# Attention and a silu MLP in one kernel: score units of the late visits one place earlier, one couple's q in rows of its own, late weight loads issued by GpSimd

## The chip, the cores and the metric

The kernel runs on one core of one Trainium2 chip. The metric is device time in microseconds (us). Engines are named as in the profile: PE is TensorE's matmul, PEld its weight load, DVE is VectorE, ACT is ScalarE, POOL is GpSimd, and SP is SyncE, which only issues DMAs. `L706` is line 706 of the kernel before.

## The reference

The inputs are `q`, `k`, `v` (8 batches, 12 heads, 448 tokens, 64 wide), two gains, and the weights `w_in` (768 x 2048) and `w_out` (2048 x 768), all float32.

```python
q_n, k_n = rmsnorm(q, g_q), rmsnorm(k, g_k)          # over the 64 of a head
attn = softmax(q_n @ k_n.T / sqrt(64))               # per batch and head
x = (attn @ v).transpose(0, 2, 1, 3).reshape(3584, 768)
h = x @ w_in                                         # 3584 x 2048
out = (h * sigmoid(h)) @ w_out                       # 3584 x 768
```

## The kernel before

**Couples.** Attention is done in 24 couples of four heads each (two pairs of heads of one batch); three couples make a batch, and six couples (`GROUP`) a group of two batches, whose x is then multiplied by w_in. The code counts couples from 0, so that couple 8 of the change's short name is `c = 7` in the code; the code's count is used from here on. The main loop is

```python
for c in range(NC):
    visit(c)
    between(c)
visit(NC)
```

**A visit** holds the attention of couple c. It has seven score units, `scores(c, j, i)` for j = 0, 1, 2 (blocks of 128 keys) and i = 0, 1 (the pair), and one for the 64 keys left over (`LEFT`). A unit is four matmuls (L701) into a PSUM tile named `sc`, of which there are two, and the exponentials on ACT (L706). The products with v, `weigh(c, j, step)`, are matmuls (L738) into two PSUM banks, `av0` and `av1`, one of each. A visit begins by finishing the couple before: the last products of c-1, a small copy into a bank (`turn`, L714), and `divide(c-1)` (L796, DVE), which multiplies the banks by the reciprocals of the softmax sums and so writes x. Only after the divide may the first products of couple c enter the banks. "Late" visits are those with c of 6 and more; in the earlier ones PE transposes q and k.

**Between two visits** lie, on PE, mostly the products of w_in with the x of a previous group (L870, PSUM tiles `mm`, two of them), a fast matrix multiplication with seven products for eight. Their sums go through DVE (L828), POOL (L890, L891) and ACT (L888, L1008), and the finished blocks are saved to a DRAM tensor `hidden` (SP, L903) from whose landing on a staging tile is free again. Other steps are dealt out among these products, in an order that the program writes out by hand; there is no planner:

- `add` (L752, DVE) and `sum_up` (L772 PE, L781 DVE): sums of the exponentials and their reciprocals, which SP then spreads over the partitions by DMAs (L787, L789).
- `flip(c+1, "q")` and `flip(c+1, "k")` (L644, L647, DVE): transposes of the next couple's q and k. After the flip of q, its rows are free, and the flip issues the next loads into them (`load_q`, L249, eight DMAs of 56 KB on SP).
- `sum_squares(c+2)` (ACT L661, DVE L662) and `scale(c+2)` (PE L673, DVE L674, POOL L677 and L680): the RMS norm of the q of the couple after the next, in place.
- the norm of k (ACT L458, DVE L459 and L483, POOL L487).
- `weights_in`: a piece of w_in, 128 x 512, is rounded. A `Rounder` loads it (L84), ACT splits it (L99, L100), DVE rounds (L122, L125, L129) and POOL adds (L133); at the end of a rounding the next loads are issued whose raw tile is free. A raw tile is free after the rounding before it that used it.
- `sum_x` (L825, DVE): sums of x that the fast multiplication needs, once a group and bank half.

Each engine takes its instructions in the order of the program. Between(c) for c = 6 and up holds 52 or 56 product matmuls. Couple c's q lies in `q_of(c)`: two sets of rows in turn for c below 6, one alone, `rows_q[0]`, from 6 on:

```python
def q_of(c):
    return rows_q[c % 2 if c < GROUP else 0]
```

So in between(5), q(6) is flipped, q(7) is loaded over it, and then squared and scaled before visit 6. After all visits the rest of the w_in products follow, and from 890 us on the products with w_out (L1177, L1214), which the change doesn't touch.

Of the kernel before, what the change touches and what calls it, by code (L numbers as in the profile page):

```python
# [17 lines left out]
I64 = mybir.dt.int64  # L18
# [45 lines left out]
class Rounder:  # L64
# [3 lines left out]
    def __init__(self, nc, pieces):  # L68
        self.nc = nc
        self.pieces = pieces  # L70
        self.loaded = self.opened = self.rounded = 0

    def load(self):

        i = self.loaded
        if i == len(self.pieces):
            return False
        dst, src, raw, low = self.pieces[i]
        if raw[0] is not None and raw[0] >= self.rounded:
            return False  # L80
        self.loaded += 1
        raw = raw[1]
        if src.dtype == I64:
            self.nc.sync.dma_start(raw.bitcast(I64), src)  # L84
        return True

    def open(self):
# [439 lines left out]
def bounded(  # L527
# [10 lines left out]
    NC, loads, place, norm, spare, ones, first, squares = (  # L538
        own[name] for name in ("NC", "loads", "place", "norm", "spare", "ones", "first", "squares")
    )  # L540
    GROUP = z.NPAIR
# [45 lines left out]
        return own["second_q"] if c == 1 else raw_q[c % 2]  # L587

    def q_of(c):
        return rows_q[c % 2 if c < GROUP else 0]  # L590

    def load_q(c):

        if 0 < c < NC:
            loads["q"](c, raw_of(c) if c < GROUP else q_of(c))
# [15 lines left out]
    def transpose_q(c):  # L611

        t = ps.tile([P, 2, BANK], F32, name="sc", bufs=2)
        both = [t[:, i] for i in range(2)]
        if c == 0:
            both[1] = ps.tile([P, BANK], F32, name="av1")
        for i in range(2):
            for j in range(J):
                rows = q_of(c)[0:R, ts(i * J + j, 2 * D)]
                nc.tensor.transpose(both[i][:, ts(j, R)], rows, ident[0:R, 0:R])  # L620
            if c == 0:
                (nc.scalar.copy, nc.vector.tensor_copy)[i](qT[:, i], both[i][:, 0:S])
        if c > 0:
            nc.scalar.copy(qT, t[:, :, 0:S])
        if c == GROUP - 2:
            load_q(GROUP)

    def transpose_k(c):

# [11 lines left out]
    def flip(c, name):  # L641

        if name == "q":
            nc.vector.transpose(qT.rearrange("p i s -> p (i s)"), q_of(c)[:, 0 : z.NK])  # L644
            load_q(c + 1)
            return
        nc.vector.transpose(kT, place["k1"])  # L647
        if c + 1 < NC:
            loads["quarters"](c + 1)
# [7 lines left out]
    def sum_squares(c):  # L657

        if c >= NC:
            return  # L660
        nc.scalar.activation(squares, q_of(c)[:, 0 : z.NK], AF.Square)  # L661
        nc.vector.tensor_reduce(  # L662
            out=norm.rms[c % 2][:, 0:n], in_=squares.rearrange("p (n e) -> p n e", e=z.Q),
            axis=AX.X, op=ALU.add,
        )
# [26 lines left out]
    def scores(c, j, i=None):  # L692


        two = ps.tile([P, 2, BANK], F32, name="sc", bufs=2)
        for half in range(2):
            pair = half if j == LEFT else i
            keys = kT[:, ds((z.KA, z.KB)[0 if j == LEFT else i] + j * P, P)]
            for h in range(2):
                rows = ds(h * D, D)  # L700
                nc.tensor.matmul(  # L701
                    two[ds(half * D, D), h, 0:S], keys[rows, ts(half, D)], qT[rows, pair, :],
                    start=True, stop=True,
                )
        for h in range(2):
            nc.scalar.activation(  # L706
                eleft[:, h] if j == LEFT else weights(c, j)[:, i, h], two[:, h, 0:S], AF.Exp,
                scale=norm.column(c, i, h, j),
            )
# [638 lines left out]
    def weights_in(c, half):  # L1348
        i = 2 * (c - GROUP) + half
        work = [step_of[step] for step in ("ro" if c < GROUP else halves.get(i, ""))]  # L1350
        return work + [lambda a=a: sum_w_in(*a) for a in sums_halves.get(i, ())]
# [10 lines left out]

    def visit(c):

        if c < GROUP - 1:
            beside = normalise(c + 1)
        elif c == GROUP - 1:
            beside = [lambda: sum_squares(c + 1), lambda: scale(c + 1)] + normalise(c + 1)[2:]
        else:
            beside = []  # L1370
        if c < NC:
            scores(c, 0, 0)
        run_all(beside[0:1])
        if c > 0:
            weigh(c - 1, LEFT)
            weigh(c - 1, LEFT - 1, 0)
            turn(1, nc.scalar.copy if c < GROUP else nc.vector.tensor_copy)
        if c < NC:
            scores(c, 0, 1)
        if c == 0:  # L1380
            run_all(beside[1:2])
        if c > 0:
            weigh(c - 1, LEFT - 1, 1)
            if c - 1 < EARLY:
                for i in range(2):
                    nc.vector.tensor_copy(x_of(c - 1, i), sums[i])
                run_all(beside[1:2])
                if inverting:
                    if c > 1:
                        divide(c - 2, None)  # L1390
                    run_all(inverting)
                    inverting.clear()
            else:
                divide(c - 1, sums)
                run_all(beside[1:2])
                if c < NC and c % GROUP == 0:
                    for i in range(0 if c == GROUP else 1, HW):
                        sum_x(last_two(c), i)
                weights_in_visit(c)
            if c + 1 < NC:  # L1400
                loads["vrest"](c + 1)
        if c == NC:
            return
        scores(c, 1, 0)
        scores(c, 1, 1)
        if c < GROUP:
            run_all(beside[2:3])
        weigh(c, 0, 1)
        scores(c, 2, 0)
        weigh(c, 1, 1)  # L1410
        turn(0, nc.scalar.copy)
        if c < GROUP:
            run_all(beside[3:4])
        scores(c, 2, 1)
        weigh(c, 0, 0)
        run_all(add(c, 1))
        weigh(c, 1, 0)
        scores(c, LEFT)
        if c + 1 < NC:
            loads["v"](c + 1)  # L1420

    def run_all(work):
        for piece in work:
            piece()

    def between(c):

        def transposes_and_sums():
            summing = sum_up(c)
            if c < GROUP:  # L1430
                next(summing)
            if c < GROUP - 1:
                transpose_k(c + 1)
            reciprocals = next(summing)
            if GROUP - 1 <= c < NC - 1:
                reciprocals += [lambda: flip(c + 1, "k"), gain]
            if GROUP // 2 <= c <= EARLY:
                divide(c - 1, None)
            return reciprocals

        if c < GROUP - 1:
            transpose_q(c + 1)
        elif c < NC - 1:
            flip(c + 1, "q")
        if c < GROUP // 2:
            inverting.extend(transposes_and_sums())
        elif c == GROUP - 1:
            run_all(transposes_and_sums())
        if c >= GROUP and c % GROUP == 0:
            fetched = range(AHEAD) if c == GROUP else ()  # L1450
            columns = products - 2 * HW * S * len(fetched)
            work = halves_in(last_two(c), range(HF), plain_in, dict(begun), fetched)
            begin(work, columns, 2 * GROUP)
            begun.clear()
        late = add(c, LEFT - 1) + add(c, LEFT) if c >= GROUP else []
        further = normalise(c + 2)[2:] if c >= GROUP - 1 else []
        queries = [lambda: sum_squares(c + 2)] if c >= GROUP - 1 else []
        fill(late + weights_in(c, 0) + further)
        prompt = transposes_and_sums() if GROUP // 2 <= c != GROUP - 1 else []
        if c == GROUP // 2:  # L1460
            begin(make_ahead([0, 1]), AHEAD * 2 * HW * S, GROUP - 1)
        fill(weights_in(c, 1), prompt[:3] + [lambda: run_all(prompt[3:] + queries)])
        if c == GROUP - 2:
            pair_up()
        if c % GROUP == GROUP - 1:
            finish()
            if c == GROUP - 1:
                begun[0] = fetch_ahead([0, 1], 0)
            else:
                sum_x([c // GROUP * 2, c // GROUP * 2 + 1], 0)  # L1470
        if c >= GROUP - 1:
            scale(c + 2)
        if GROUP <= c < NC - 1:

            nc.scalar.activation(first, minus_half, AF.Exp)
        if c == NC - 1:
            while rounder.load():
                pass
# [236 lines left out]
```

## Time and profile before

| what | value |
|---|---|
| median of 3 runs | 1343.11 us (1342.66 to 1343.29) |
| profiled execution, own time | 1346.0 us |
| its span | 1344.1 us |
| mean granted PE clock of it | 0.994 |
| busy PE / DVE / ACT / POOL | 1300.4 / 951.8 / 502.3 / 369.5 us |
| visit 6 | 131.36 to 144.79 us |
| visit 7 | 168.85 to 179.85 us |
| visit 8 | 203.38 to 214.36 us |
| visit 9 | 243.42 to 254.40 us |

The visits' times are from PE's timeline: from the first matmul of unit (0, 0) on. The profile comes from one execution, and its times are from the span's start. In a timeline a row has start, length, engine, line, operation, output <- input, and in brackets how long the engine was idle before it and what released it. "SPq" rows are DMAs being issued, which takes SP's time; the transfer lands later. The clock of PE is granted by a throttle, and a matmul at half clock takes about twice as long.

### The profile page before, as it was taken

To read this page: it belongs to the slowest core of one execution; us is meant where nothing else is said; L and a number is where in the kernel's file an instruction comes from. 1 tells how busy PE (TensorE), PEld (TensorE's weight loads), DVE (VectorE), ACT (ScalarE), POOL (GpSimd) and SP (SyncE) were. 2 spreads that over 40 slices of the span, in tenths; PEclk is the share of its full clock that TensorE was granted. 3 is DMA by queue.
4 is the path that set the end of the run, shared out by engine and by line. 5 is a ranking of instruction groups with operands and counts; after the bars stand their busy time and mean duration, and the time that the engine had idled before them with its cause. 6 is when DMAs were issued, how large, how long until landed. Compare 5 with 4: busy or idle time off the path is not lost.

```text
span 1344.1 us, 19812 instructions
## 1 busy us (share of the span) xinstructions
PE 1300.4 (97%) x7111; PEld 828.3 (62%) x7111; DVE 951.8 (71%) x1630; ACT 502.3 (37%) x877; POOL 369.5 (27%) x223
## 2 busy tenths in 40 slices
PE   8997998999999999999999999999999999999997
PEld 4332443444444444444444455557999999999997
DVE  5786876785855655855554586789978787878785
ACT  7874455556445545455544244420000000101000
POOL 5765344443343343343331044410000000000000
PEclk9998999999999999999999999999999999999999
DMA  8565456434433543443421257422323232332311
GB/s 230 155 147 123 119 155 161 106 89 109 108 91 88 124 93 87 124 97 86 112 74 38 101 176 262 149 98 71 103 75 99 75 102 77 99 100 79 125 48 39
DMA packets 286543, 147.69 MB, mean 110 GB/s; under 512 B 224420, under 2 KB 270372, under 8 KB 286436
## 3 DMA queue, kind: packets, MB, share of 16 engines
q1 hardware_dynamic: 285872, 145.35, 39.6%
q8 instruction: 58, 0.95, 0.3%
q0 software_dynamic: 256, 0.79, 0.2%
q14 instruction: 49, 0.40, 0.1%
q10 hardware_dynamic: 308, 0.20, 0.0%
HBM read 96.73 MB, written 41.29 MB: 103 GB/s over the span
## 4 chain that ended last, share of the span: by engine, by line
PE 81%; DVE 7%; ACT 4%; DMA 3%; issue 2%; SPq 2%; POOL 0%; ACTq 0%; DVEq 0%
PE mm L870 24%; PE alone L1177 22%; PE av L738 8%; PE sc L701 8%; PE mm L1177 7%; PE alone L870 7%; PE alone L1214 2%; DVE work L781 1%; DVE work L752 1%; DMA rows<-in_k_dram 1%; PE sc L772 1%; SPq L249 1%; DVE sums_x L825 1%; PE mm L1214 1%; ACT L1008 1%
## 5 line engine op out<-in xcount | busy, mean ns | idle before, releaser
L870 PE MATMUL mm<-x,W 128*128 128x448 f32 x636 | 258.6, 549 | 12.0 <-DVE parts L828 3.3
L706 ACT ACTIVATE work<-sc,rms 128x448 f32<-128x448 f32 x324 | 185.5, 635 | 86.2 <-PE sc L701 62.8
L870 PEld LDWEIGHTS mm<-x,W 128*128 128x128 f32 x636 | 117.6, 191 | 146.8 <-issue 114.7
L870 PE MATMUL mm<-sums_x,W 128*128 128x448 f32 x456 | 186.5, 548 | 6.8 <-DVE parts L828 4.8
L701 PE MATMUL sc<-work 64*64 64x448 f32 x1344 | 167.3, 550 | 1.7 <-DVE rms L674 1.1
L738 PE MATMUL av<-work,rows 64*64 64x448 f32 x1296 | 156.0, 546 | 4.7 <-ACT av L714 1.8
L752 DVE TENSOR_TENSOR work<-work 128x896 f32<-128x896 f32 (+1 forms) x114 | 123.7, 1115 | 49.4 <-PE av L738 48.8
L870 PEld LDWEIGHTS mm<-sums_x,W 128*128 128x128 f32 x456 | 85.1, 191 | 100.2 <-issue 83.4
L487 POOL TENSOR_TENSOR rms<-rms,minus_half 128x14 f32<-128x14 f32 (+3 forms) x37 | 88.3, 2389 | 134.6 <-DVE rms L483 133.9
L514 POOL DMA_DIRECT2D out_dram<-x x2 | 1.3, 652 | 443.0 <-DVE x L828 443.0
L1177 PE MATMUL alone<-W,rows 128*128 128x192 f32 x608 | 113.0, 326 | 0.0
L738 PEld LDWEIGHTS av<-work,rows 64*64 64x64 f32 x1296 | 60.7, 133 | 76.0 <-issue 35.4
L677 POOL TENSOR_TENSOR rms<-rms,minus_half 128x28 f32<-128x28 f32 x18 | 86.2, 4791 | 74.7 <-DVE rms L674 63.3
L1177 PEld LDWEIGHTS alone<-W,rows 128*128 128x128 f32 x608 | 101.2, 190 | 0.0
L701 PEld LDWEIGHTS sc<-work 64*64 64x64 f32 x1344 | 55.5, 134 | 69.1 <-ACT work L706 26.9
L890 POOL TENSOR_TENSOR parts<-parts,stage 128x448 f32<-128x448 f32 x31 | 42.0, 1355 | 150.3 <-DVE parts L828 149.9
L1177 PE MATMUL alone<-W,work 128*128 128x192 f32 x382 | 72.2, 326 | 0.0
L1008 ACT ACTIVATE stage<-stage 128x896 f32<-128x896 f32 x63 | 57.4, 947 | 24.7 <-DVE stage L828 24.1
L1177 PEld LDWEIGHTS alone<-W,work 128*128 128x128 f32 x382 | 63.8, 190 | 0.0
L1187 ACT COPY rows<-alone 128x192 f32<-128x192 f32 x34 | 10.9, 320 | 137.4 <-PE alone L1177 78.9
L781 DVE RECIPROCAL work<-sc 128x224 f32<-128x224 f32 x36 | 55.6, 1547 | 5.2 <-PE sc L772 5.0
L459 DVE TENSOR_REDUCE rms<-rows 128x8 f32<-128x512 f32 (+2 forms) x48 | 30.2, 629 | 40.3 <-ACT rows L458 37.5
(243 smaller groups left out, 2104.9 us busy)
## 6 DMA issues: line engine op xcount, KB each, us to landing
hidden<-stage SPq DMA_DIRECT2D x63, 448.0 KB, 3.1
work<-hidden SPq DMA_DIRECT2D x21, 1024.0 KB, 5.1
rows<-in_moe_w_out_dram SPq DMA_DIRECT2D x32, 384.0 KB, 3.4
W<-in_moe_w_in_dram SPq DMA_DIRECT2D x22, 512.0 KB, 5.0
work<-work SPq DMA_DIRECT2D x144, 56.0 KB, 2.0
rows<-in_q_dram SPq DMA_DIRECT2D x144, 56.0 KB, 2.3
rows<-in_k_dram SPq DMA_DIRECT2D x144, 56.0 KB, 2.4
x<-hidden SPq DMA_DIRECT2D x7, 1024.0 KB, 5.6
```

The costliest lines, as they stand in the source:

```text
L487: nc.gpsimd.tensor_tensor(out=t, in0=t, in1=half, op=ALU.pow)
L677: nc.gpsimd.tensor_tensor(out=f, in0=f, in1=minus_half.to_broadcast([P, n]), op=ALU.pow)
L701: nc.tensor.matmul(two[ds(half * D, D), h, 0:S], keys[rows, ts(half, D)], qT[rows, pair, :], start=True, stop=True,)
L706: nc.scalar.activation(eleft[:, h] if j == LEFT else weights(c, j)[:, i, h], two[:, h, 0:S], AF.Exp, scale=norm.column(c, i, h, j),)
L738: nc.tensor.matmul(sums[i][ds(h * D, D), :], v, w, start=(j == 0 and step == 1), stop=(j == LEFT - 1 and step == 1),)
L752: nc.vector.tensor_tensor(out=total, in0=total, in1=more, op=ALU.add)
L781: nc.vector.reciprocal(out=r[0][:, rows], in_=t[:, rows])
L870: nc.tensor.matmul(t, self.left(name, s), self.right(name, s), start=s == ends[0], stop=s == ends[1])
L890: nc.gpsimd.tensor_tensor(out=u2, in0=u2, in1=p5, op=ALU.add)
L1008: nc.scalar.activation(t, t, AF.Silu)
L1177: nc.tensor.matmul(t, x[:, i], y, start=i == ORDER[0], stop=i == ORDER[-1])
L1214: nc.tensor.matmul(o, a[:, 2 * i + m, t], right_one(name, i)[:, m], start=n == 0, stop=n == len(steps) - 1,)
```

## The change

It has three parts.

1. In late visits `scores(c, 1, 0)` is issued before the last product of couple c-1 (and so before the divide), and `scores(c, 2, 0)` before the first product of couple c. PE's order before was: 00, two products of c-1, 01, last product of c-1, 10, 11, product 0, 20, product 1, 21, and so on. Now: 00, two products of c-1, 01, 10, last product of c-1, 11, 20, product 0, product 1, 21.
2. Couple 7's q goes to the second set of rows, which is free by then, and is loaded in between(4). Its squares and scale are no longer at the end of between(5); they are dealt among the first products of between(6), with `sum_squares` where the flip of q(7) stood, and that flip comes late in between(6), after the flip of k. In between(5) the flip of q(6) is followed by the load of q(8).
3. From visit 6 on, the loads of w_in (seven into W tiles and two into an x tile, 512 KB each) are issued by POOL instead of SP, directly after POOL's rounding instruction in POOL's order.

```diff
@@ class Rounder
+        self.queue = nc.sync
...
-            self.nc.sync.dma_start(raw.bitcast(I64), src)
+            self.queue.dma_start(raw.bitcast(I64), src)
@@ def q_of(c)
-        return rows_q[c % 2 if c < GROUP else 0]
+        return rows_q[c % 2 if c < GROUP + 2 else 0]
@@ def transpose_q(c)
-        if c == GROUP - 2:
-            load_q(GROUP)
+        if c >= GROUP - 2:
+            load_q(c + 2)
@@ def flip(c, name)
-            load_q(c + 1)
+            if c != GROUP + 1:
+                load_q(c + 2 if c == GROUP else c + 1)
@@ def visit(c)
+        if c == GROUP:
+            room.w_in.queue = nc.gpsimd
...
+        if GROUP <= c < NC:
+            scores(c, 1, 0)
         if c > 0:
             weigh(c - 1, LEFT - 1, 1)
...
-        scores(c, 1, 0)
+        if c < GROUP:
+            scores(c, 1, 0)
         scores(c, 1, 1)
         if c < GROUP:
             run_all(beside[2:3])
+        if c >= GROUP:
+            scores(c, 2, 0)
         weigh(c, 0, 1)
-        scores(c, 2, 0)
+        if c < GROUP:
+            scores(c, 2, 0)
@@ def between(c)
+            if c == GROUP:
+                reciprocals.insert(3, lambda: flip(c + 1, "q"))
...
-        elif c < NC - 1:
+        elif c < NC - 1 and c != GROUP:
             flip(c + 1, "q")
...
-        queries = [lambda: sum_squares(c + 2)] if c >= GROUP - 1 else []
-        fill(late + weights_in(c, 0) + further)
+        queries = [lambda: sum_squares(c + 2)] if c >= GROUP else []
+        prompt = [lambda: sum_squares(c + 1), lambda: None, lambda: scale(c + 1)]
+        fill(late + weights_in(c, 0) + further, prompt if c == GROUP else [])
...
-        fill(weights_in(c, 1), prompt[:3] + [lambda: run_all(prompt[3:] + queries)])
+        n = max(3, len(prompt) - 1)
+        fill(weights_in(c, 1), prompt[:n] + [lambda: run_all(prompt[n:] + queries)])
...
-        if c >= GROUP - 1:
+        if c >= GROUP:
             scale(c + 2)
```

## The prediction

> **What bounds the kernel now.** I read the page's busy times first, then TensorE's waits in the stretch that the change touches, then the queues behind those waits.
>
> ```profile
> PE 1300.4 (97%) x7111; PEld 828.3 (62%) x7111; DVE 951.8 (71%) x1630; ACT 502.3 (37%) x877; POOL 369.5 (27%) x223
> ```
>
> TensorE (PE) is the bound. The change adds and removes no matmul, so only time in which PE waits, or runs at half clock, can move. After 760 us the two programs are alike. PE's waits between 100 and 345 us, in total, count and longest:
>
> ```profile
> PE mm L870 <- DVE parts L828: 7.0, 6, 2.0
> PE mm L870 <- DVE stage L828: 4.7, 6, 1.2
> PE sc L673 <- DVE rms L662: 4.7, 3, 3.9
> PE mm L870 <- ACT stage L888: 3.2, 2, 2.5
> PE mm L870 <- DVE work L781: 2.4, 1, 2.4
> ```
>
> The 3.9 us is couple 7's sum of squares, late at the end of between(5). PE's timeline (start, length, instruction, idle before):
>
> ```profile
> 122.76 4.12 PE L870 MATMUL mm<-x,W 128*128 128x448 f32 x6 [2.38 <-DVE work L781]
> 130.80 0.62 PE L673 MATMUL sc<-rms,ident 128*128 128x28 f32 x2 [3.92 <-DVE rms L662]
> 131.36 1.03 PE L701 MATMUL sc<-work 64*64 64x448 f32 x4
> ```
>
> The 2.5 us at L888 lies in between(8). SP's timeline there, then ACT's line from the timeline of all engines:
>
> ```profile
> 213.00 3.51 SPq L84 DMA_DIRECT2D W<-in_moe_w_in_dram  x2
> 219.65 2.31 SPq L303 DMA_DIRECT2D rows<-in_v_dram  x4
> 222.05 4.07 SPq L249 DMA_DIRECT2D rows<-in_q_dram  x8
> 226.22 0.90 SPq L903 DMA_DIRECT2D hidden<-stage  x2
> ```
>
> ```profile
> 229.50 0.53 ACT L888 COPY stage<-mm 128x448 f32<-128x448 f32 x1 [8.56 <-DMA hidden<-stage]
> ```
>
> Until 216.6 SP is at w_in loads that wait for roundings on POOL (SP's waits name L133: 14.5 us in four waits from 100 to 345 us). The v and q loads and the save of `hidden` queue behind them. The save is issued at 226.22 though its activation ended near 219.8; L888 waits for it, L458 and L459 wait behind L888, and a product behind L459 costs PE another 2.02 us at 234.62.
>
> In the late visits themselves little is lost: 11.00 us (visit 7) against 28 rounds of four matmuls side by side, 0.376 us each, 10.52. That is 0.45 to 0.51 per visit; visits 12 and 18 lose 1.31 and 1.26.
>
> **What the Trainium skill says.** "TensorE: Matmul & The Clock Gate", Part 1, gives a free-running window of 3413 ns after which an idle PE runs at half clock. The trace agrees: the records show half clock from 122.64 to 126.05, from 129.47 to 136.29 and from 235.28 to 238.69, one or two such windows each, after the waits shown. "SBUF — State Buffer", section "SBUF: two separate sides", calls the port pair of VectorE and GpSimd an exclusive lock, and its box warns that a DMA of the POOL queue has descriptors made by GpSimd, which the lock can keep waiting. Of the first the trace shows L125, 0.43 us mostly and up to 1.80; of the second only POOL's stores at the kernel's end, 0.54 to 0.76 us each.
>
> **Part 1, couple 7's q.** L661, L662, L673 and L674 leave between(5). Its last products then end at 122.76 + 4.12 = 126.9, and visit 6 starts there, 4.5 us sooner than 131.36; the second half-clock window (131.36 to 136.29 inside the visit, worth 2.46) goes too.
>
> Three things take some back. SP issues q(8)'s eight loads (0.52 us each, some 4.2 to 4.9 in all) in the slot of q(7)'s, but q(7)'s eight have gone in earlier, into a queue nearly without gaps from 99 to 129. So the spreading of couple 5's reciprocals (L787, L789) comes that much later: the last L789, issued by 128.9 before, is issued near 132 to 133 and landed at about 134.5. The divide (L796, 137.90 before) can't start sooner; PE would have its banks full at 132.5, and waits some 1.7 us at the first product into a bank not yet divided. The score unit moved forward waits for the first exponential, behind L99 and L100 on ACT (0.4), and a product waits for the copy L714 behind DVE's rounding (0.6). Visit 6: 126.8 + 10.5 + 0.45 + 0.4 + 0.6 + 1.7 = 140.4, where it ended at 144.8: **4.4 ahead**.
>
> In between(6) the work comes back. After the divide, DVE has the sums of x and the adds to 144.4; ACT squares after the last exponentials (144.5 to 145.45), L662 ends at 146.6, L828 and two L752 follow, and L674 ends at 150.3. POOL then works in order. Durations are those of POOL's groups:
>
> - L677 4.8, L680 1.7, L133 1.3, w_in load 0.65 (the stores' price), L890 1.14: together 9.6.
>
> L890 thus ends at about 160.0. The L828 that waits for it started at 158.78 before, now at 160.1: 1.3 later. PE has two product buffers and idles about 4 us meanwhile. Behind that L828 stands what it had behind it, plus the flip of couple 7's q (L644), 1.10, which stood at 148.9. Visit 7 therefore starts 1.3 + 1.1 = **2.4 later** than 168.85, less 0.1 for DVE's idle spots: +2.3. So 4.4 us won at the visit's end are lost in the stretch. Bounds: −2, if the spreading is not late and the chain starts with it; +5, if the load's descriptors wait for DVE (the box gives about 3.1 us for one beside a VectorE copy; no run here shows it) and PE falls to half clock.
>
> **Part 2, w_in loads by POOL.** Seven W and two x loads of 512 KB go. SP is rid of the wait for L133, since POOL issues the load after its own rounding. In between(8) the v and q loads and the save run through, and L888 comes about 22 us after visit 8's start at 203.38, some 4 before its 26.1. The wait of 2.55 goes; of 2.02 stay about 1.6; the half-clock window, 1.7, goes; and of the 1.03 at 221.7 some 0.4. In sum 2.55 + 0.4 + 1.7 + 0.4 = **−5.1**; from −2.5 (another engine late next: DVE, busy 27 of 40 us there) to −5.5. On POOL a load costs 0.65 ahead of L890, with POOL 27% busy it hides, but for between(6) above. Landing (5.0 before) may grow by the issue; the load is needed two roundings later, so at nothing; if that cover is gone, PE waits for a rounding, 1 to 2 us.
>
> **Part 3, score units forward.** Nothing is added. In a visit, unit 20 comes 1.5 us sooner and waits for the exponential of 10 to free its "sc" buffer (+0.28), while two staggers (0.2 at the product 11, 0.1 at 00 behind L714) vanish: about −0.03 in each of 12 visits, ±0.2 each. Four visits whose first exponential is late gain 0.25 of waiting each, visits 12 and 18 the same: +1.5 in all, less 0.4, about **+1.2**. In between(7) and between(9) the divide ends 0.75 later, because its last product is one unit later, and DVE's adds with it: +0.6 and +0.4. Visit 12 and 18's own loss (0.8 each, waiting L674) may shrink: −0.4.
>
> **Sum:** +2.3 − 5.1 + 1.2 + 0.6 + 0.4 − 0.4 = −1.0. Against the profiled execution's own 1346.0 us that is 1345.0; the median of the runs, 1343.11, lies 2.9 lower, so 1342.1, no difference a measurement can tell (it tells about 0.2%, 2.7 us).
>
> **The rivals.** *Visit 6's gain is kept.* Then POOL's chain is not what between(6) ends on: for it speaks that in the trace of before POOL idled 16.15 us ahead of L133 there, so that the pow and multiply have room if L674 comes 2 us earlier; against it, DVE is busy 21.5 of the 24 us from 145 to 169. It gives −4.4 + 1.1 of the flip for +2.3, the sum then −1.0 − 5.6 = −6.6: 1336.5.
>
> *POOL becomes the bound, and it ends slower.* Place: POOL's order in between(6), pow, multiply, rounding, load, L890. Price: PE's idle passes 3.4 us, so that a half-clock window follows (1.7), and the load's issue takes 3.1 for 0.65 (+2.5); elsewhere the loads wait too, 1 us in two stretches. Sum −1.0 + 1.7 + 2.5 + 2 = +5.2: 1348.3. It decides from the point at which the load is issued beside VectorE's two-input adds.
>
> *The order of the units costs every visit*: 0.3 in each of 17 more than I take, +5: 1347, if unit 20's wait stands and the staggers don't go. *The loads on POOL do nothing*, because SP's later loads are held by something else: between(8) keeps its 8.6 us of stall, and the sum is +4.1: 1347.2.
>
> **How the numbers follow.** My forecast 0.42 (its own range 1339.5 to 1345: 0.27 within the bound, 0.10 faster, 0.05 slower); the gain kept 0.28 (all but 0.02 faster); POOL the bound 0.15, slower; the other two 0.15 (0.12 slower, 0.03 within). Together 0.36 faster, 0.32 within, 0.32 slower. The range runs from 1335.5, just below the second case, to 1348.5.
>
> **What would show each step.** Visit 6 should start near 127 with no wait at L673; its first products into undivided banks wait for L796 near 134.5; L890 in between(6) ends near 160 with PE idle 4 us before; visit 7 starts near 171. In between(8) L903 follows its activation within a microsecond, L888 has no long wait, and there is no half clock. Plain visits stay within 0.2 of 11.0. I am wrong if visit 7 starts before 167 or after 174, if POOL's loads take over 2 us to issue, or if the visits from 13 on change by over 0.2 each.

## The result, and the profile after

The changed kernel takes 1346.99 us (median of 16 runs, 1344.66 to 1348.22) against 1343.96 (16 runs, 1342.43 to 1344.83): ratio 1.0022, 95% interval 1.0015 to 1.003. It is slower by about 3 us, a little more than what a measurement can tell. The forecast was 1342.1, about 1 us faster and too little to be measured, with 1335.5 to 1348.5 as its range: the time lies inside the range, but on the other side of the kernel before.

Lines after the change have moved by one or two: L84 is now L85, L133 L134, L677 L679, L680 L682, L828 L830, L888 L890, L890 L892, L903 L905. The page's busy times after:

```profile
PE 1295.8 (96%) x7111; PEld 810.0 (60%) x7111; DVE 950.2 (71%) x1630; ACT 500.7 (37%) x877; POOL 376.3 (28%) x232
```

POOL has nine instructions and 6.8 us more, the loads among them. PE's waits between 100 and 345 us, as total, count and longest:

```profile
PE mm L872 <- DVE stage L830: 10.9, 8, 4.8
PE mm L872 <- DVE parts L830: 5.7, 5, 2.0
PE sc L675 <- DVE rms L664: 2.6, 4, 1.7
PE sc L703 <- ACT work L708: 1.8, 1, 1.8
PE av L740 <- DVE x L798: 1.4, 1, 1.4
PE mm L872 <- ACT stage L890: 0.6, 1, 0.6
```

Two waits that the change aimed its edits at are gone: the 3.9 at couple 7's sum of squares, and the 2.5 at L888, now L890 (0.6). In their place stands one of 4.8 us behind L830, where the longest of that kind was 1.2. It is in between(6). Two shorter ones are new in visit 6: 1.8 for the first exponential (L708) and 1.4 for the divide (L798). PE's timeline in visit 6 and between(6):

```profile
133.52 1.88 PE L740 MATMUL av<-work,rows 64*64 64x448 f32 x14 [1.43 <-DVE x L798]
138.71 4.78 PE L872 MATMUL mm<-sums_x,W 128*128 128x448 f32 x12
160.34 7.08 PE L872 MATMUL mm<-sums_x,W 128*128 128x448 f32 x12 [4.75 <-DVE stage L830]
171.72 0.98 PE L703 MATMUL sc<-work 64*64 64x448 f32 x8
```

Visit 6 ends at 138.7, products follow, and then PE stands for 4.75 us. The twelve matmuls after it take 7.08 us where twelve before it take 4.78: half clock. (The clock's records show it from 158.18 to 165.01; the 4.67 us of this in which PE was at work, at half the speed, make the 2.3 us of difference.) What L830 waits for is on POOL's timeline:

```profile
148.71 5.69 POOL L679 TENSOR_TENSOR rms<-rms,minus_half 128x28 f32<-128x28 f32 x1 [17.33 <-DVE rms L676]
154.47 1.69 POOL L682 TENSOR_TENSOR x<-x,rms 128x896 f32<-128x896 f32 x1
156.12 1.28 POOL L134 TENSOR_TENSOR W<-W 128x512 int32<-128x512 int32 x1
157.71 0.76 POOL L85 DMA_DIRECT2D W<-in_moe_w_in_dram  x1 [0.31 <-POOL W L134]
158.49 1.14 POOL L892 TENSOR_TENSOR parts<-parts,stage 128x448 f32<-128x448 f32 x1
```

and from DVE's timeline, an addition that runs when the pow begins, and the instruction that L892 holds:

```profile
148.66 1.09 DVE L754 TENSOR_TENSOR work<-work 64x896 f32<-64x896 f32 x1
159.66 0.62 DVE L830 TENSOR_TENSOR stage<-mm,parts 128x448 f32<-128x448 f32 x1 [7.15 <-POOL parts L892]
```

POOL was idle for 17.33 us, then the pow, the multiply, the rounding and the load stand ahead of L892 for 9.8 us. DVE idles 7.15 us and PE 4.75 behind it. Before the change only the rounding stood there; from POOL's timeline, then DVE's:

```profile
156.37 1.29 POOL L133 TENSOR_TENSOR W<-W 128x512 int32<-128x512 int32 x1 [16.15 <-DVE W L129]
157.61 1.14 POOL L890 TENSOR_TENSOR parts<-parts,stage 128x448 f32<-128x448 f32 x1
```

```profile
158.78 0.62 DVE L828 TENSOR_TENSOR stage<-mm,parts 128x448 f32<-128x448 f32 x1 [1.43 <-POOL parts L890]
```

**Where the time went.** The two profiled executions start differently: visit 5, which the change doesn't touch, begins 1.47 us sooner in the second. The differences below are counted from there, after less before, as the visits' starts and ends in PE's timelines give them.

| point | difference by then, us | forecast's step |
|---|---|---|
| start of visit 6 | -6.2 | -4.5 |
| end of visit 6 | -4.6 | -4.4 |
| start of visit 7 | +4.3 | +2.3 |
| start of visit 8 | +4.9 | +2.9 |
| start of visit 9 | +0.2 | -2.2 |
| start of visit 10 | +1.1 | (not given apart) |
| start of visit 23 | +2.1 | -1.0 (the end) |

After visit 23 the programs are alike. The trace thus gives +2.1, the medians of the runs +3.0. The two profiled executions as a whole took 1346.0 and 1346.22 us, since the one of before is 2.0 above the median of its kernel and the other 0.8 below its own: they tell where time moved, not how much slower the kernel is. The rest I can't assign, since PE's half-clock windows fall differently in each execution (below); one that an execution has and another of the same kernel need not have is called drawn.

### The profile page after: what moved, and what is told of

It reads as the page before. It is cut to its first block, busy times and chain, and to the rows that moved or that the text cites. A ratio compares the mean times of both kernels' runs of the same rounds, so it can differ in the third digit from the quotient of the medians.

```text
span 1344.4 us, 19811 instructions
## 1 busy us (share of the span) xinstructions
PE 1295.8 (96%) x7111; PEld 810.0 (60%) x7111; DVE 950.2 (71%) x1630; ACT 500.7 (37%) x877; POOL 376.3 (28%) x232
## 4 chain that ended last, share of the span: by engine, by line
PE 78%; DVE 7%; ACT 6%; issue 4%; DMA 3%; SPq 2%; POOL 1%; ACTq 0%; DVEq 0%; POOLq 0%
PE mm L872 23%; PE alone L1179 22%; PE mm L1179 7%; PE alone L872 7%; PE av L740 7%; PE sc L703 7%; PE alone L1216 2%; ACT work L708 2%; DVE work L783 1%; DMA rows<-in_k_dram 1%; DVE work L754 1%; PE sc L774 1%; SPq L250 1%; PE mm L1216 1%; DMA hidden<-stage 1%
## 5 line engine op out<-in xcount | busy, mean ns | idle before, releaser
L708 ACT ACTIVATE work<-sc,rms 128x448 f32<-128x448 f32 x324 | 183.4, 633 | 80.3 <-PE sc L703 53.5
L703 PE MATMUL sc<-work 64*64 64x448 f32 x1344 | 158.8, 545 | 5.5 <-ACT work L708 3.5
L754 DVE TENSOR_TENSOR work<-work 128x896 f32<-128x896 f32 (+1 forms) x114 | 123.8, 1116 | 40.9 <-PE av L740 40.3
L740 PE MATMUL av<-work,rows 64*64 64x448 f32 x1296 | 143.3, 538 | 6.1 <-ACT av L716 1.8
L679 POOL TENSOR_TENSOR rms<-rms,minus_half 128x28 f32<-128x28 f32 x18 | 87.2, 4843 | 91.7 <-DVE rms L676 82.4
L740 PEld LDWEIGHTS av<-work,rows 64*64 64x64 f32 x1296 | 52.0, 132 | 80.4 <-issue 47.1
L703 PEld LDWEIGHTS sc<-work 64*64 64x64 f32 x1344 | 46.7, 132 | 83.5 <-ACT work L708 36.3
L892 POOL TENSOR_TENSOR parts<-parts,stage 128x448 f32<-128x448 f32 x31 | 42.2, 1362 | 149.0 <-DVE parts L830 141.9
L1189 ACT COPY rows<-alone 128x192 f32<-128x192 f32 x34 | 10.8, 317 | 137.5 <-PE alone L1179 79.0
L1193 ACT COPY rows<-alone 128x192 f32<-128x192 f32 x34 | 10.8, 318 | 122.5 <-PE alone L1179 118.9
```

The lines of the kernel that those rows point to most:

```text
L679: nc.gpsimd.tensor_tensor(out=f, in0=f, in1=minus_half.to_broadcast([P, n]), op=ALU.pow)
L703: nc.tensor.matmul(two[ds(half * D, D), h, 0:S], keys[rows, ts(half, D)], qT[rows, pair, :], start=True, stop=True,)
L708: nc.scalar.activation(eleft[:, h] if j == LEFT else weights(c, j)[:, i, h], two[:, h, 0:S], AF.Exp, scale=norm.column(c, i, h, j),)
L740: nc.tensor.matmul(sums[i][ds(h * D, D), :], v, w, start=(j == 0 and step == 1), stop=(j == LEFT - 1 and step == 1),)
L754: nc.vector.tensor_tensor(out=total, in0=total, in1=more, op=ALU.add)
L892: nc.gpsimd.tensor_tensor(out=u2, in0=u2, in1=p5, op=ALU.add)
```

## The experiments

Each was timed against the kernel before on the same chip. In these series and the first one the kernel before had medians of 1343.82 to 1344.06, so medians of different series are compared as they are. "Trace" is the difference to the kernel before at the start of visit 23, counted from visit 5 as above.

| kernel | median, us | ratio (95%) | trace, us |
|---|---|---|---|
| part 1 alone | 1346.80 | 1.0027 (1.0018 to 1.0037) | +1.6 |
| part 2 alone | 1339.78 | 0.9972 (0.9962 to 0.9982) | -4.5 |
| part 3 alone | 1348.79 | 1.0040 (1.0026 to 1.0054) | +1.8 |
| parts 1 and 2 | 1343.64 | 0.9999 (0.9990 to 1.0007) | -0.4 |
| parts 2 and 3 | 1343.59 | 1.0004 (0.9995 to 1.0012) | -1.1 |
| all, scale(7) late | 1343.22 | 1.0004 (0.9996 to 1.0012) | -1.4 |
| parts 1 and 2, scale(7) late | 1342.67 | 0.9988 (0.9977 to 1.0000) | -5.4 |
| the same, spreading first | 1341.82 | 0.9982 (0.9974 to 0.9990) | -5.0 |
| unit (1,0) alone | 1354.18 | 1.0078 (1.0064 to 1.0092) | +7.8 |
| unit (2,0) alone | 1350.19 | 1.0055 (1.0041 to 1.0069) | +3.8 |
| all, w_in loads of between(6) on SP | 1348.95 | 1.0044 (1.0030 to 1.0058) | +2.7 |
| part 2 from visit 8 on | 1341.28 | 0.9979 (0.9971 to 0.9987) | -4.5 |

**Each part by itself.** The edits are those of the diff above, one part at a time.

> Part 1 alone: couple 7's q in rows of its own; the loads of w_in stay with SP and the score units where they were. Theory (POOL's order in between(6): pow 5.7, multiply 1.7, rounding 1.3 and only then L890): PE waits 3.5 to 4 us at a product behind L890, the load's 0.76 + 0.31 us on POOL being gone; visit 7 starts 2.5 to 3.3 later than before, counted from visit 5's start, and the total is +2 to +3.5 us (1346 to 1347.5 against 1344). Rival A (the load on POOL is what holds L890): visit 7 at most 1 later, total within 1 us. Rival B (the score order makes the loss): total 3 or more faster, since between(5) is 6 us shorter.

Part 1 alone is 2.9 us slower, and visit 7 starts 2.8 later: the theory's range. Its POOL timeline has the same chain without the load:

```profile
149.85 5.69 POOL L678 TENSOR_TENSOR rms<-rms,minus_half 128x28 f32<-128x28 f32 x1 [17.56 <-DVE rms L675]
157.27 1.28 POOL L133 TENSOR_TENSOR W<-W 128x512 int32<-128x512 int32 x1
158.51 1.12 POOL L891 TENSOR_TENSOR parts<-parts,stage 128x448 f32<-128x448 f32 x1
```

Here 8.66 us pass from the pow to the sum (L891 in this kernel), 1.12 fewer than with the load. PE waits 2.79 there, less than expected, because it came there later: it had waited 0.80 and 1.45 for DVE, and the twelve matmuls behind that had run partly at half clock (6.47 us for 4.78). Rivals A and B fall.

> Part 2 alone: w_in loads of visit 6 and later issued by POOL. Theory: between(8) loses 4 to 5 us of stall (29.1 to about 24.5), between(6) at most 1 us longer through the 0.7 us load ahead of L890, total -3.5 to -5 us (about 1339.5). Rival A (loads on POOL cost in other stretches what they give in between(8)): within 1 us of before.

Part 2 alone is 4.1 us faster, as the theory had it. Between(8) is 24.0 us for 29.1. (The 29.1 is long: the four other profiles with these loads on SP have 26.6 to 28.1 there, so that the traces show a gain of 2.6 to 5.1.) SP's timeline there, then ACT's:

```profile
216.97 4.80 SPq L250 DMA_DIRECT2D rows<-in_q_dram  x8
221.88 0.90 SPq L904 DMA_DIRECT2D hidden<-stage  x2
```

```profile
224.70 0.53 ACT L889 COPY stage<-mm 128x448 f32<-128x448 f32 x1 [4.94 <-DMA hidden<-stage]
```

The v loads are out by 214.6 and the save no longer follows loads of w_in. L889 still waits, but no longer PE for it: counted from visit 8's start (202.23) it runs at 22.5, before the change at 26.1.

> Part 3 alone: units (1,0) and (2,0) one place forward in visits 6 and later. Theory: visits 7 and on keep 11.0 us within 0.05, visits 12 and 18 0.15 longer, between(7) and between(9) 0.4 to 0.9 longer since the divide and DVE's adds come one unit later; total +1 to +2.5 us. Rival B: each visit 0.2 longer, total +4 or more. Third possibility: no change within 0.5.

Part 3 alone is 4.9 us slower; its trace shows +1.8. The next visit's start comes 0.66 later over visit 7 and between(7), and 0.88 over visit 9 and between(9), and the plain visits stay within 0.1 of 11.0, visits 17 and 23 apart (11.23 and 11.14), as expected. After visit 23 the trace loses 2.8 us more for another reason, seen in PE's timeline at the end of attention, here of the kernel before and then of this one:

```profile
760.06 4.75 PE L870 MATMUL alone<-x,W 128*128 128x448 f32 x12 [1.37 <-DVE x L796]
```

```profile
760.45 7.71 PE L870 MATMUL alone<-x,W 128*128 128x448 f32 x12 [1.37 <-DVE x L796]
```

Both wait 1.53 and 1.37 us just before, and one is then at half clock and the other not: 2.96 us that no edit made. The difference at visit 23 leaves this one out, but not those earlier (part 3 alone has four half-clock stretches between 121 and 300 us, the kernel before three), and the median of the runs holds them all. I take +1.8 to +4.9 for part 3 alone, and leave it there.

**Two parts of three.**

> Parts 1 and 2 without part 3: the changed kernel with the old order of score units. Theory (the three costs add, and part 3 is worth +2 by its trace, up to +5 by its times): 1342 to 1345, that is 2 to 5 us under the changed kernel, with PE's wait of about 4.5 us at the product behind L890 still there. Rival (part 3 costs nothing beside the other two, as a version with a late scale suggests, 1343.2 with and 1342.7 without it): within 1 us of the changed kernel.

> Parts 2 and 3 without part 1: couple 7's q stays where it was. Theory (part 1 is a loss of 2.9 by itself): 3 us under the changed kernel, 1342.5 to 1344.5. By its trace between(5) has its 3.9 us wait at L673 again and between(6) none above 2 us. Rival (part 1's loss comes only with the load on POOL): within 1 us of the changed kernel.

Without part 3, and likewise without part 1, the kernel is at 1343.6, 3.4 us under the changed kernel and level with the kernel before: both rivals fall. Between(6) keeps its wait of 4.8 in the first. In the second the wait at the sum of squares in between(5) is back, 5.5 us long (PE came to it sooner, with no half clock at 122 us), and between(6) has none above 2.33. The three costs alone sum to 2.9 - 4.1 + 4.9 = +3.7, near the +3.0 of all together: part 2's gain is real, and parts 1 and 3 each spend most of it.

**POOL's order in between(6).** Same kernel as changed, but scale(7) is dealt later:

```diff
-        prompt = [lambda: sum_squares(c + 1), lambda: None, lambda: scale(c + 1)]
+        prompt = [lambda: sum_squares(c + 1)]
...
+        if c == GROUP:
+            prompt.insert(1, lambda: scale(c + 1))
```

> The changed kernel with scale(7) dealt after the first products of between(6) rather than among them, so that on POOL the pow and the multiply stand behind L890, L891 and the pow of k instead of ahead of the rounding, the load and L890. Theory: L890 of between(6) starts near 153.5 instead of 158.5, the wait of 4.75 on PE falls below 1.5, no half clock follows, visit 7 starts 5 to 7 us sooner than in the changed kernel, total -4.5 to -7 us against the changed kernel (1340 to 1342.5). Rival C (DVE's work bounds between(6) whatever POOL's order): at most 1.5 us sooner. If the multiply is then late for the flip of q(7), half of the gain is left.

3.8 us under the changed kernel, 1343.22 for 1346.99, a little less than expected; visit 7 starts 5.0 sooner. POOL's timeline:

```profile
151.37 0.76 POOL L85 DMA_DIRECT2D W<-in_moe_w_in_dram  x1 [0.31 <-POOL W L134]
152.15 1.15 POOL L892 TENSOR_TENSOR parts<-parts,stage 128x448 f32<-128x448 f32 x1
157.30 4.78 POOL L679 TENSOR_TENSOR rms<-rms,minus_half 128x28 f32<-128x28 f32 x1
```

L892 starts at 152.15 for 158.49, with the same load ahead of it, and the pow is 4.78 us long. PE has no wait above 2.74 in between(6), and one of 2.10 at the end of it, at the next sum of squares, which is late in turn. The theory's 1.5 without half clock did not come: half clock follows the 2.74 (from 150.42), and visit 7 draws another window (12.7 us long), so that of the 5.0 us 3.9 are left at the start of visit 8. DVE's work did not bound the stretch: rival C falls.

> Parts 1 and 2 without part 3, with scale(7) dealt after the first products of between(6). Theory (the three costs add): 1343.2 of the version with all three and late scale, less what part 3 costs, 3 to 5 us: 1338.5 to 1340.5, at or a little below part 2 alone (1339.8). Rival (between(6) is bound by DVE's work once POOL's order is mended, so part 1 brings nothing): 1339.8 within 0.5, and visit 7 starts no sooner than with part 2 alone.

1342.67, above the theory's range and above part 2 alone, though its trace lies 0.9 below that one at visit 23. Its profile has a half-clock spell at the end of attention, as part 3 alone has. In its 13 runs the two fastest, 1338.2 and 1338.4, had a mean PE clock of 0.998 and the slowest, 1346.0, one of 0.992. Neither theory nor rival is decided by this.

The next has q(8)'s loads taken out of the flip of q(6) and moved behind the spreading:

```diff
-                load_q(c + 2 if c == GROUP else c + 1)
+                if c != GROUP:
+                    load_q(c + 1)
...
             run_all(transposes_and_sums())
+            load_q(c + 3)
```

> The same, and the eight loads of q(8) in between(5) are issued after the spreading of couple 5's reciprocals. Theory (the spreading stands behind these loads on SP, so the divide of visit 6 is late): the last L789 is issued 4 to 5 us sooner, PE's wait at the first product into an undivided bank in visit 6 goes, visit 6 ends 1 to 2 us sooner, total -1 to -2 us against the version without this. Rival (DVE's sums of x are next, and bound between(6) anyway): within 0.5 us.

The last pair of L789's kind is issued from 125.50 on, where it was 130.15, and PE's wait for the divide (0.30 in that kernel) is gone; visit 6 ends 0.85 us sooner, a little less than expected. The median moves by 0.85 with ranges that overlap: not told from nothing. In the trace visit 7 starts 1.3 sooner, but draws a half-clock window (12.7 us long for 11.0), and by the start of visit 8 the gain is gone.

**Which unit costs.**

> Only unit (1,0) of the late visits goes ahead of the last product of the couple before; the rest as before the change. Theory (the divide and DVE's adds come one unit, 0.75 us, later, and the products of between(7) and between(9) wait for DVE): between(7) 0.6 and between(9) 0.8 us longer, nearly all of what all of part 3 costs, total +2 to +4.5 us. Rival (it is unit (2,0), whose PSUM buffer waits for an exponential): within 0.7 us of before.

> Only unit (2,0) of the late visits goes ahead of the first product of its couple. Theory: its wait for the exponential of (1,0) and the staggers that vanish cancel, visits stay at 11.0 us, total within 1 us of before. Rival: +2 to +4 us.

Both theories are wrong: the totals are 10.1 and 6.1 us over the kernel before. Either unit alone makes nearly every late visit longer: 11.5 us with (1,0), 11.45 with (2,0), where both together, as the kernel before, have 11.0. PE's timeline in visit 14 with (2,0) alone:

```profile
418.34 0.98 PE L701 MATMUL sc<-work 64*64 64x448 f32 x8 [0.54 <-ACT work L706]
```

With three units in a row, the third waits for an exponential to free its PSUM buffer, 0.54 us. With (1,0) alone the same visit shows matmuls in twos and fours in place of eights, with no single wait on the list; what holds them is not shown. The two moves mend each other; that is the cancelling which the forecast took as given.

**Loads on POOL, where.** The switch of the queue moves by one or two visits:

```diff
-        if c == GROUP:
+        if c == GROUP + 1:
             room.w_in.queue = nc.gpsimd
```

> The changed kernel, but the w_in loads of between(6) stay with SP; POOL issues only those from visit 7 on. Theory: POOL's chain ahead of L890 is shorter by the load (0.76) and the gap before it (0.31), L890 starts 1.1 sooner, visit 7 starts 1 us sooner (2 if the half-clock window after PE's wait is not drawn), total -1 to -2 us against the changed kernel. Rival (the load on POOL keeps L890 for longer than it runs): -3 or more.

The local step came out: from the pow to L892 it is 8.65 us for 9.78, and PE waits 3.60 for 4.75. But the twelve matmuls after the wait take 7.75 us for 7.08, more of them being at half clock, and visit 7 starts only 0.2 sooner. The total is 1348.95, 2 us over the changed kernel. In this profile visit 6 drew a half-clock window (15.4 us long), and between(8) is 0.7 longer: the eight q loads ahead of the save took SP 5.50 us for 4.72, and the save and L890 came that much later. The theory's -1 to -2 is not confirmed, and the rival's -3 is refuted.

> Part 2 alone, cut to its working half: POOL issues the w_in loads only from visit 8 on, before that SP. Theory (all of part 2's gain is SP's freed queue in between(8)): 1339 to 1340, as part 2 alone (1339.8) or up to 1 us less, since between(6) keeps its order of before. Rival (part of the gain lies in between(6) and (7)): 1341 or more.

With `GROUP + 2` on part 2 alone the trace is at -4.5 as with all of part 2: its gain is in between(8) (23.9 us), and the loads of visits 6 and 7 add nothing to it. Between(6), 1.2 longer in the trace of part 2 alone, is as long here, where its loads stay with SP, so they are not what lengthens it. The runs are at 1341.28, 2.5 faster than before, which falls to the rival's side. Part 2 alone has the lowest median of all, 1339.78; the intervals of the two versions overlap, so the times don't tell them apart. The trace speaks against the rival: visits 7 and 8 start 0.6 later than before the change, not sooner.

## Why the prediction was wrong, point by point

**Between(5) and visit 6: the end right, the way there not in all.** The end of visit 6 was to come 4.4 us sooner, and comes 4.6 sooner. The wait for the divide was put at 1.7 and is 1.43. The start was to come 4.5 sooner; it came 6.2 sooner in three of the profiles with part 1 and 4.5 to 4.6 in four, which, like the kernel before, have a half-clock window at 122 us. In the changed kernel's profile the 1.7 us of this went into the wait for the first exponential, 1.82 where 0.4 was forecast. The end doesn't depend on it, since PE waits for the divide in any case, and the divide came when it was forecast.

**Between(6): the mechanism right, two terms of the sum wrong.** By the traces this is the step that failed: the chain on POOL ahead of L890 was summed too small, and the half clock after PE's wait was left out of the sum. Between(6) was to give the gain back to +2.3, and did so to +4.3.

- The chain ahead of L890 was summed as 4.8 + 1.7 + 1.3 + 0.65 + 1.14 = 9.6. It measures 5.69 + 1.69 + 1.28 + 0.76 + 1.14, and 0.4 of gaps, that is 10.9. The largest miss is the pow. It begins beside the VectorE addition L754, which has two inputs in SBUF. "SBUF — State Buffer", "SBUF: two separate sides", calls the port pair of the two engines an exclusive lock for this pairing. The traces agree: this addition has 1.04 us to go when the pow begins, and the pow is 0.9 longer. Of the 252 pows of this shape in the fourteen traces four begin during this addition, and they take 5.69; the other 248 take 4.78 to 4.82. The load's price was nearly right, 0.76 for 0.65, plus the 0.31 before it.
- The half clock after PE's wait was priced at 1.7 and put into a rival with a chance of 0.15. With an idle of over 4 us forecast it belonged in the sum. Between L830's start and visit 7 pass 12.06 us for 10.07; 1.1 of the 2.0 is the flip, as forecast, and the other 0.9 is PE's slow matmuls, for which DVE in turn waits 0.85 and 0.35 us. "TensorE: Matmul & The Clock Gate", Part 1, has windows of 3413 ns: an idle of 4.75 us puts at least 2.37 us into one of two neighbouring windows, however they fall, and 2.05 was enough at the end of attention with part 3 alone (half clock from 759.6 us; the window before it holds the wait of 1.53 and 0.52 of the next). So that window could not be missed, and 3.41 us of half clock were to be counted at the least; it lasted 6.83 (from 158.18).

The chain's 1.3 less 0.2 (L674, now L676, ended so much sooner than forecast) and 0.9 for the clock make the 2.0.

**Between(8): right in the place, 0.4 short, and perhaps not all of it the change's.** -5.1 was forecast, -4.7 came: L890 at 22.85 from visit 8's start (22 forecast), no half clock. But the save was to follow its activation within a microsecond and L888 to have no long wait; the save is issued 3.2 us after it, behind the q loads, and L890 still idles 5.03 us. It is PE that no longer waits for it. The 1.7 for the half-clock window counts one that the profile of before had drawn, which not every run of that kernel need have; the medians of part 2 give -4.1, and -2.5 from visit 8 on.

**Part 3: right for the wrong reason, and small.** +1.8 in sum was forecast. All three parts less parts 1 and 2 give +2.5 by the traces, 0.75 of it in between(9) where 0.4 stood, and +3.35 by the medians (+4.9 for part 3 alone). So by the medians part 3 is a miss of 1.6 to 3.1 us, as large as between(6) or larger; why its runs cost more than its trace stays open. Visits at 11.0 hold only because the two moves compensate; the claim for each is refuted.

**Sum.** -1.0 was forecast. Between(6) adds 2.0, between(8) 0.4, part 3 0.7: +2.1, which is the trace. The rival that kept visit 6's gain fell with the start of visit 7. The rival "POOL becomes the bound" had the place and the engine; its further terms, a load of 3.1 us and loads waiting elsewhere, didn't come, so its +5.2 was too much. (The 3.1 us stands on the cited page not in the box but in the part after it, "A bandwidth-pool intuition that's wrong (but worth ruling out)", and is for a copy.) The rival with the loads doing nothing is refuted by part 2 alone.

## What to carry to other kernels

When a step is moved off a late wait, list everything that stands behind it in the in-order queue where it lands, and sum that queue to the next instruction which another engine waits for. If the sum leaves PE idle for some 4 us or more, put the half-clock window into the sum and not beside it (an estimate, twice the 1.94 us of the next section); for 2 to 4 us it depends on where the windows fall. Try the parts of a combined change singly and in pairs: here one part is worth 4.1 us, and the two others take it back; each half of one of them lengthens the late visits, which both together leave as they were.

## What the runs showed of the hardware that was not expected

- Waits that don't change between two kernels can cost 3 us in one execution and nothing in the other, since a half-clock window falls on them or not (760 us: twelve matmuls in 4.75 or 7.71 us after the same two waits).
- How much idle time draws half clock can be read from the traces. In the twelve of the fourteen that have more than one half-clock stretch in this part, the stretches begin whole multiples of 3.413 us apart (the kernel before: 122.64, 129.47, 235.28), so from any one of them the windows can be laid over the whole trace and PE's idle time counted in each (from its records, whose ends are modelled). Between 95 and 1300 us all 33 full-clock windows with 1.94 us of idle or more are followed by half clock, and of those with less only three, with 1.70 to 1.87; the largest idle that was not followed by it is 1.86. In a window at half clock less idle is enough to stay there for the next: 0.71 us or more did so in all 13 cases, and with 0.32 or less it ended in all 36.
- Runs of one kernel spread by up to 8 us (parts 1 and 2 with late scale, 1338.2 to 1346.0), those of part 2 alone by 1.4 and of part 2 from visit 8 on, with a trace that is nearly the same, by 4.7. What decides the spread is not shown.
- A 512 KB load from POOL's queue took 0.53 to 0.76 us of POOL and landed in 4.5 us (median of nine, 3.9 to 6.8), beside 5.0 (3.6 to 6.7) for the same loads from SP before the change. The long issue beside VectorE, of which the prediction kept 3.1 us as an end of its range, showed in none of the nine. Two of them were issued while the addition L754 ran (220.15 and 220.69 us, taking 0.55 and 0.53), none beside a copy within SBUF, which is the case that the 3.1 us is for.
